# Transposing the last two blocks' normalised tiles: from TensorE to 32x32 squares by DMA and VectorE, with three sums of w2's rows at other units

## The chip, the cores and the metric

The kernel runs on one core of a Trainium2 chip. Its time is the device time of one execution in microseconds (us). The time before is the median of three runs. A profile is one further execution, recorded instruction by instruction; it has a time of its own, and a span from its first to its last instruction.

## The reference, cut to what matters

One transformer block with modulation, on x of 2048 tokens by 512 channels, all in float32:

```
mod = silu(c) @ w_mod -> sa, ca, ga, sb, cb, gb          # six rows of 512
h = layernorm(x) * (1 + ca) + sa
x = x + ga * (linear_attention(h @ wqkv) @ wo)           # 32 heads of 16
h = layernorm(x) * (1 + cb) + sb
x = x + gb * (mish(h @ w1 + b1) @ w2)                    # 512 -> 1792 -> 512
```

The change is about the second layernorm's h, on its way into `h @ w1`, and about w2.

## The kernel before

**Blocks and passes.** The 2048 tokens are four blocks of 512, each of four tiles of 128 tokens by 512 channels. `b` names the block, `t` the tile of tokens, `j` a group of 128 channels, `f` one of the 14 groups of 128 hidden columns of w1 (`NF`), `g` a pair of these (7, `G`). All matrix products run on TensorE in pieces of float32r: each operand is split into a high half (ScalarE, L82) and a low half (VectorE, L88), and `mm3` (L72) makes three matmuls of a product. Several products use seven multiplications in place of eight; that is why sums and differences of operands are prepared (`rows` for w1, `columns` for the normalised activations, `w2_sums` for w2's rows).

**The MLP.** Blocks 0 and 1 go through `h @ w1` together, then blocks 2 and 3. `pair_unit` (L1146) does one pair `g` for two blocks at once: seven products of six matmuls, and two `between` units. For blocks 0 and 1 the pairs run in the loop at L1244. Beside them `trail(f)` (L1230) multiplies the finished hidden columns of block 0 with w2 (`d_unit`, L1067, twelve matmuls). After the loop come the trails of f = 11, 12, 13 (L1258), and then `second(1, prepare)` (L1261): fourteen units of twelve matmuls each for block 1, in the order `last_first` (f = 10 to 13, then 0 to 9). `prepare(f)` (L1201) is called at the start of each such unit. Then the last stage begins: `pair_begin` and `two_pairs` for blocks 2 and 3 (L1382), and the w2 products of these blocks.

**The normalised tiles of blocks 2 and 3.** `norm_tile(b, t)` (L918) normalises one tile of tokens in place and stores it to a DRAM tile `nd` (POOL's queue, L937), two tiles in each of the units g = 2 to 5. After the last pair of the loop, `load_back` (L939) loads the eight tiles again as `nb` (SP's queue). The product with w1 needs them with channels on partitions. `transpose_f` (L945) does that: four TensorE transposes of 128x128 into one PSUM bank, then one ScalarE activation that applies scale and shift and writes `hf`. `prepare` calls it twice in each of the units 1, 3, 5 and 7 of `second`. In units 4 and 8 it starts `columns`, which reads four `hf` each and makes the operands of the seven products.

**Sums of w2's rows.** `w2_sums(g)` (L695) loads two row groups of w2 from DRAM (`w2p`, L700) where `g` is below 5, makes four differences on VectorE (L710), splits them, and stores the halves to DRAM (`w2t`, L726, four stores on SP). `W2_AT` (L693) says in which unit of `second` which `g` is started. `load_wt` (L1348) reads `w2t` when the seventh pair of the last stage begins and later.

**Order.** The instructions of each engine run in the order in which this program issues them. Side work is written as generators: `spawn` adds one that advances at every `tick`, up to its next `yield`; `spawn_idle` adds one to a list of which only the first two (three in the last stage) advance. So `prep_a` (L1178), which splits the activations for `second`, puts its ScalarE half into one tick and its VectorE half into the next. SBUF tiles come from one pool of 101 buffers; a tile waits for the last use of the buffer that it is given.

Of the kernel before, what the change touches and what calls it, by code (L numbers as in the profile page):

```python
# [8 lines left out]
F32 = mybir.dt.float32  # L9
# [4 lines left out]
P = 128  # L14
# [11 lines left out]
def block_kernel(ctx: ExitStack, tc: tile.TileContext, x, wqkv, wo, w1, b1t, w2, c, wmodt, out):  # L26
# [11 lines left out]
    def sb(name, dt=F32, shape=(P, 512)):  # L38

        return big.tile(list(shape), dt, tag="T", name=name, bufs=SLOTS)  # L40
# [12 lines left out]
    def spawn_idle(gen):  # L53

        idle_work.append(gen)

    def tick():

        running.extend(fresh)
        fresh.clear()  # L60
        for g in list(running):
            if next(g, "end") == "end":
                running.remove(g)
        for g in idle_work[:width[0]]:
            if next(g, "end") == "end":
                idle_work.remove(g)
# [623 lines left out]
            pool.dma_start(w2f[g][:, n, :], t)  # L690

    w2t, w2k, wb = {}, {}, {}
    W2_AT = {0: 6, 1: 5, 2: 0, 3: 1, 6: 2}  # L693

    def w2_sums(g):  # L695

# [43 lines left out]
    def rows(g, wait):  # L740

        r = [sb(f"w1p_{g}_{i}", F32, (P, 4, P)) for i in range(2)]
        for i in range(2):
            f = 2 * g + i
            sp.dma_start(r[i], w1[:, P * f:P * (f + 1)].rearrange("(k p) f -> p k f", p=P))
        for _ in range(wait):
            yield
        a11, a12, a21, a22 = [r[i][:, 2 * k:2 * k + 2, :] for i in range(2) for k in range(2)]
        s12, s34 = [sb(f"s{n}_{g}", F32, (P, 4, P)) for n in (12, 34)]
        s1, s2, s3, s4 = s12[:, 0:2, :], s12[:, 2:4, :], s34[:, 0:2, :], s34[:, 2:4, :]  # L750
        dve.tensor_tensor(s1, a21, a22, op=ALU.add)
        dve.tensor_tensor(s2, s1, a11, op=ALU.subtract)
        dve.tensor_tensor(s3, a11, a21, op=ALU.subtract)
        dve.tensor_tensor(s4, a12, s2, op=ALU.subtract)
        yield
        keep, todo = {}, []
        op_rows[g] = keep
        for name, v, parts in (("a1", r[0], ("a11", "a12")), ("s12", s12, ("s1", "s2")), ("s34", s34, ("s3", "s4")),
                               ("a22", a22, ("a22",))):
            half = split(f"{name}_{g}", v, keep, name)  # L760
            next(half)
            todo.append((name, half, parts))
            if len(todo) == 2:
                yield
                for name, half, parts in todo:
                    run(half)
                    for i, part in enumerate(parts):
                        op_a[g, part] = [h[:, 2 * i:2 * i + 2, :] for h in keep[name]]
                todo = []
# [148 lines left out]
    def norm_tile(b, t):  # L918

        v = xt.pop(("r", b, t))  # L920
        if t % 2:
            ln_stats("n", b, t, v)
            ln_eps("n", b, t, t + 1)
            ln_rstd("n", b, t, t + 1)
            yield
            ln_apply("n", b, t, v, v, dve)
        else:
            sums = act_sums("n", b, t, v)
            yield
            sums_eps("n", b, t, sums)  # L930
            yield
            sums_shift("n", b, t, sums)
            yield
            ln_apply("n", b, t, v, v, act)
        yield
        d = nd[b, t] = drp.tile([P, D], F32, name=f"nd_{b}_{t}")
        pool.dma_start(d, v)  # L937

    def load_back(key, src, b, t):  # L939
        v = xt[key, b, t] = sb(f"{key}b_{b}_{t}")  # L940
        sp.dma_start(v, src.pop((b, t)))

    hf, op_b = {}, {}

    def transpose_f(b, j, ptag="tp"):  # L945
        p = ps(ptag, f"tp_n_{b}_{j}")
        for t in range(4):
            pe.transpose(p[:, P * t:P * (t + 1)], xt["n", b, t][:, P * j:P * (j + 1)], ident)  # L948
        hf[b, j] = sb(f"hf_n_{b}_{j}")
        act.activation(hf[b, j], p, AF.Identity, bias=mc[:, 12 + j:13 + j], scale=mc[:, 16 + j:17 + j])  # L950
# [4 lines left out]
    def columns(c0, c, done):  # L955

        b11, b12, b21, b22 = [hf.pop((b, c + h)) for h in (0, 2) for b in (c0, c0 + 1)]
        t = [sb(f"t_{c0}_{c}_{i}") for i in range(4)]
        for d, u, v in (t[0], b12, b11), (t[1], b22, t[0]), (t[2], b22, b12), (t[3], b21, t[1]):
            dve.tensor_tensor(d, u, v, op=ALU.subtract)  # L960
        yield
        names = [("b11", b11), ("b21", b21), ("t1", t[0]), ("t2", t[1]), ("t3", t[2]), ("t4", t[3]), ("b22", b22)]
        halves = [split(f"{name}_{c0}_{c}", v, op_b, (name, c)) for name, v in names if name not in done]
        for n in range(0, len(halves) + 2, 2):
            for h in halves[max(n - 2, 0):n] + halves[n:n + 2]:
                next(h, None)
            yield
# [132 lines left out]
    def pair_begin(c0, g, tags):  # L1100

        u1, pa = sb(f"u1_{g}"), product(g, "a11", "b11", tags[0])
        act.activation(u1, pa, AF.Copy)  # L1103
        c11, p = sb(f"c11_{g}"), product(g, "a12", "b21", tags[1])

        def result():
            add(c11, p, u1)
            yield
            yield from mish(c11, c0, 2 * g)

        spawn(result())
        return pa
# [33 lines left out]
    def pair_unit(c0, g, odd, between):  # L1146
        begun = pair_begin(c0, g, ("tp" if odd else "h", "h"))
        tick()
        state = pair_early(g, begun, "h")
        tick()  # L1150
        between[0]()
        pair_middle(g, *state)
        tick()
        between[1]()
        tick()
        pair_end(c0, g, *state)
# [39 lines left out]
            spawn(prep_a(b, last_first[u - NF + 3]))  # L1196

    G = NF // 2
    order = [(b, c + h) for c in range(2) for h in (0, 2) for b in (2, 3)]

    def prepare(f):  # L1201

        if f in (1, 3, 5, 7):
            for _ in range(2):
                transpose_f(*order.pop(0), "h")
        if f in (4, 8):
            spawn_idle(columns(2, f // 4 - 1, ()))
        if f in W2_AT:
            spawn(w2_sums(W2_AT[f]))
        if f == NF - 2:  # L1210
            load_rows(0)
            load_wb(5)
        if f == NF - 1:
            load_wb(6)
# [11 lines left out]
    def norm_next():  # L1226
        if tiles:
            spawn(tiles.pop(0))

    def trail(f, side=None, norm=True):  # L1230
        def unit():
            if side is not None:
                if norm:
                    norm_next()
                spawn(side)
            d_unit(0, f, f)
            ahead(1, f)
            if f > 5 and f % 2 == 0:
                for i in (4, 5):
                    if f + i < NF:  # L1240
                        load_w2(f + i)
        return unit

    for g in range(1, G):  # L1244
        for f in (2 * g, 2 * g + 1):
            spawn(w2_job(f))
        if g == 1:
            two_pairs(0, 0, 1, begun, (lambda: None, trail(0, rows(3, 2), False)))
            store_rows(0)
        else:  # L1250
            norm_next()
            pair_unit(0, g, g % 2, (trail(2 * g - 3), trail(2 * g - 2, rows(g + 2, 2) if g + 2 < G else ())))
        if g < KEPT:
            store_rows(g)
        if g == G - 1:
            for n in range(8):
                load_back("n", nd, 2 + n // 4, n % 4)
    for f in (NF - 3, NF - 2, NF - 1):  # L1258
        trail(f)()
        tick()  # L1260
    second(1, prepare)  # L1261


# [98 lines left out]
    for n, g in enumerate(pairs):  # L1362
        if n < 5:
            if n:
                load_rows(n)
            if n:
                load_wb(pairs[n + 1])
        if n == 5:
            load_wb(pairs[6])
            load_r(0, 0)  # L1370
        if n == 6:
            for m in pairs[:5]:
                load_wt("m4", m)
        def gap(c, m):
            def unit():
                e_unit(c, m)
            return unit

        if n in (3, 5):
            spawn_idle(w2_sums(SUMS_KEPT[n // 2 - 1]))  # L1380
        if n == 0:
            begun = [pair_begin(L, pairs[i], ("tp" if i else "h", "acc")) for i in range(2)]  # L1382
            tick()
        elif n == 1:
            two_pairs(L, pairs[0], g, begun, (gap(0, 0), gap(0, 1)))
            for i in range(2):
                spawn_idle(left_trail(pairs[i]))
        else:
            pair_unit(L, g, n % 2, (gap(1, 0), gap(1, 1)) if n == 2 else (gap(0, n - 1), gap(1, n - 1)))
            if n < EARLY:  # L1390
                spawn_idle(left_trail(g))
# [70 lines left out]
```

## Time and profile before

| what | value |
|---|---|
| median of 3 runs | 493.3 us (493.01 to 493.44) |
| the profiled execution, its own time | 493.66 us |
| its span | 492.0 us |
| granted TensorE clock | 1.00 |
| busy: POOL / ScalarE / VectorE / TensorE | 146.1 / 296.4 / 370.8 / 487.3 us |
| moved by DMA | 98.58 MB in 66785 packets |
| unit g = 6 of the first pass | from about 286.3 to 301.3 us |
| trails of f = 11, 12, 13 | to 309.3 us |
| `second(1, prepare)` | 309.3 to 351.0 us |

In the profile, PE is TensorE, PEld its weight loads, DVE VectorE, ACT ScalarE, POOL GpSimd, SP SyncE; L948 is line 948. q0 is the DMA queue of POOL, q1 that of SP. A row of a timeline gives start, duration, engine, line, operation, output and input, and in brackets how long the engine was idle before and what ended that. A row of the windows gives for a stretch of time its length, then the busy time of PE, PEld, DVE, ACT and POOL with the number of instructions, the granted clock, the mean busy share of the 16 DMA engines (records overlap, so it can exceed 1), and GB/s; where it is asked for one engine, only that engine's. A row of waits gives who waited for whom, the total, the number of times and the longest.

### The profile page before, as it was taken

The numbers are of one execution on the slowest core, as the hardware profiler recorded it, in microseconds if no ns is written. First come the engines' busy times: TensorE is split into PE (matmuls) and PEld (weight loads), VectorE is DVE, ScalarE is ACT, GpSimd is POOL, SyncE is SP. The second block draws the span as 40 slices with busy tenths as digits, with TensorE's granted clock in tenths as the row PEclk, the third lists the DMA queues.
The fourth block names the chain that finished last, engine by engine and source line by source line (L and its number), as shares of the span: only waits on it lengthen the run. The fifth ranks groups of instructions, "written<-read, shape, count | busy, mean of one in ns | idle before, by whom it ended". The sixth has DMA issues, their size and how long they took to land.

```text
span 492.0 us, 7721 instructions
## 1 busy us (share of the span) xinstructions
PE 487.3 (99%) x2642; PEld 411.7 (84%) x2642; DVE 370.8 (75%) x717; ACT 296.4 (60%) x530; POOL 146.1 (30%) x244
## 2 busy tenths in 40 slices
PE   8999999999999999999999999999999999999997
PEld 7788888878878888888888888888888888899997
DVE  7988888999799698976877653789732666769872
ACT  6768587866546879738767655288045555668100
POOL 4583120000022123103432336114744410545200
PEclk9999999999999999999999999999999999999999
DMA  8815554244864417488899879999997803688512
GB/s 306 294 43 119 138 128 86 56 148 145 290 168 108 128 45 244 130 282 294 279 328 360 295 233 284 297 293 368 385 300 193 228 24 114 176 212 244 120 44 87
DMA packets 66785, 98.58 MB, mean 200 GB/s; under 512 B 7057, under 2 KB 31641, under 8 KB 66746
## 3 DMA queue, kind: packets, MB, share of 16 engines
q0 software_dynamic: 28704, 44.19, 32.8%
q1 hardware_dynamic: 37896, 53.63, 32.5%
q8 instruction: 21, 0.34, 0.3%
q10 hardware_dynamic: 146, 0.26, 0.2%
q14 instruction: 18, 0.15, 0.1%
HBM read 62.92 MB, written 33.03 MB: 195 GB/s over the span
## 4 chain that ended last, share of the span: by engine, by line
PE 96%; DVE 2%; ACT 1%; POOL 0%; ACTq 0%; issue 0%
PE p_a L1093 19%; PE p_s L1093 8%; PE oacc L75 5%; PE oacc L76 5%; PE oacc L74 5%; PE m L76 5%; PE m L75 5%; PE m L74 5%; PE o L74 3%; PE o L76 3%; PE o L75 3%; PE pq_a L371 3%; PE gacc L74 2%; PE gacc L76 2%; PE pk L76 2%; PE gacc L75 2%
## 5 line engine op out<-in xcount | busy, mean ns | idle before, releaser
L205 POOL TENSOR_TENSOR rs_n<-rs_n,half 128x1 f32<-128x1 f32 x16 | 11.4, 712 | 61.5 <-DVE rs_n L200 35.5
L1098 DVE TENSOR_TENSOR cb<-p_s,u 128x512 f32<-128x512 f32 x28 | 19.2, 687 | 13.2 <-ACT u L1134 13.2
L1128 ACT ACTIVATE u<-p_a 128x512 f32<-128x512 f32 x12 | 7.2, 599 | 28.8 <-PE p_a L1093 28.8
L1103 ACT ACTIVATE u<-p_a 128x512 f32<-128x512 f32 x14 | 8.4, 598 | 25.8 <-PE p_a L1093 25.8
L1085 ACT ACTIVATE ub<-cb,b1c 128x512 f32<-128x512 f32 x28 | 20.0, 717 | 4.9 <-DVE cb L1098 4.7
L1360 POOL DMA_DIRECT2D wt_m<-w2t x20 | 14.0, 704 | 26.8 <-DVE cb L1098 14.7
L950 ACT ACTIVATE hf_n<-tp_n,mc 128x512 f32<-128x512 f32 x16 | 11.7, 769 | 12.8 <-PE tp_n L948 12.8
L1134 ACT ACTIVATE u<-p_a 128x512 f32<-128x512 f32 x14 | 8.4, 598 | 17.0 <-PE p_a L1093 16.0
L738 POOL DMA_DIRECT2D w2b<-w2d x20 | 10.6, 540 | 23.9 <-DVE a_12l L88 5.0
L1098 DVE TENSOR_TENSOR c<-p_a,u 128x512 f32<-128x512 f32 x14 | 9.6, 689 | 8.6 <-PE p_a L1093 6.0
L850 POOL DMA_DIRECT2D rden_d<-rden x2 | 1.4, 720 | 45.7 <-DVE rden L848 45.7
L265 DVE SCALAR_TENSOR_TENSOR ku<-e_k,relu_k 128x512 f32<-128x512 f32 x15 | 10.7, 715 | 4.9 <-ACT relu_k L263 4.8
L732 POOL DMA_DIRECT2D wb<-w2d x14 | 9.9, 712 | 14.8 <-PE p_a L1093 12.4
L1062 ACT ACTIVATE u<-p_a,b1c 128x512 f32<-128x512 f32 x14 | 9.6, 687 | 6.9 <-PE p_a L1093 6.9
L262 ACT ACTIVATE e_k<-pk 128x512 f32<-128x512 f32 x15 | 8.9, 591 | 7.8 <-PE pk L76 7.8
L205 POOL TENSOR_TENSOR rs_x<-rs_x,half 128x1 f32<-128x1 f32 (+1 forms) x10 | 7.4, 746 | 19.6 <-DVE rs_x L200 18.4
L265 DVE SCALAR_TENSOR_TENSOR q<-e_q,relu_q 128x512 f32<-128x512 f32 x16 | 10.7, 684 | 3.1 <-ACT relu_q L263 3.1
L214 ACT ACTIVATE x<-x,nb_x,rs_x 128x512 f32<-128x512 f32 x13 | 10.0, 809 | 4.7 <-DVE nb_x L209 4.0
L274 POOL DMA_DIRECT2D ku<-ku x8 | 7.2, 901 | 17.6 <-DVE ku L265 17.6
L874 DVE TENSOR_TENSOR r<-o,r 128x512 f32<-128x512 f32 x16 | 10.8, 676 | 1.0 <-PE o L76 0.9
L862 DVE SCALAR_TENSOR_TENSOR q<-q,rd 128x512 f32<-128x512 f32 x16 | 10.4, 684 | 1.5 <-DMA rd<-rden_d 1.5
L785 POOL DMA_DIRECT2D a1b<-rd_a x10 | 5.4, 541 | 18.5 <-PE p_a L1093 8.1
(1620 smaller groups left out, 1972.3 us busy)
## 6 DMA issues: line engine op xcount, KB each, us to landing
wm<-in_wmodt_dram SPq DMA_DIRECT2D x24, 256.0 KB, 5.4
w2b<-w2d POOLq DMA_DIRECT2D x20, 256.0 KB, 5.4
wt_m<-w2t POOLq DMA_DIRECT2D x20, 256.0 KB, 3.9
r<-in_x_dram SPq DMA_DIRECT2D x16, 256.0 KB, 3.0
x<-in_x_dram SPq DMA_DIRECT2D x15, 256.0 KB, 4.8
w1p<-in_w_dram SPq DMA_DIRECT2D x14, 256.0 KB, 4.0
w2r<-in_w_dram SPq DMA_DIRECT2D x14, 256.0 KB, 5.9
wb<-w2d POOLq DMA_DIRECT2D x14, 256.0 KB, 5.4
```

The costliest lines, as they stand in the source:

```text
L74: pe.matmul(o, st[0], mv[0], start=start, stop=False)
L75: pe.matmul(o, st[0], mv[1], start=False, stop=False)
L76: pe.matmul(o, st[1], mv[0], start=False, stop=stop)
L205: pool.tensor_tensor(y, y, half[:, lo:hi], op=ALU.pow)
L265: dve.scalar_tensor_tensor(dst, e, 1.0, r, op0=ALU.min, op1=ALU.add)
L371: pe.matmul(p, l, r, start=onto is None and c == 0 and i == 0, stop=c == 1 and i == 2, skip_group_check=onto is not None)
L874: dve.tensor_tensor(r, p, r, op=ALU.add)
L950: act.activation(hf[b, j], p, AF.Identity, bias=mc[:, 12 + j:13 + j], scale=mc[:, 16 + j:17 + j])
L1085: act.activation(u, p, AF.Mish, bias=b1c[:, f:f + 1])
L1093: pe.matmul(p, st, mv, start=onto is None and c == 0 and i == 0, stop=c == 1 and i == 2, skip_group_check=onto is not None)
L1098: dve.tensor_tensor(out, p, u, op=ALU.add)
L1360: pool.dma_start(v, w2t[g][:, :, SUM[name], :])
```

## The change

The tiles of one block go to one DRAM tile of 512 tokens. `load_squares(b)` reads them again in 16 DMAs for each block: a DMA fills 32 partitions of a tile `y` with 16 squares of 32x32, so that one VectorE transpose, which turns every 32x32 square in its place, gives the tile with channels on partitions (`turn`). ScalarE applies scale and shift in place. Block 2 is read before the last pair of the first pass, block 3 after it. The eight `turn`s start two in each of the trails of f = 11, 12 and 13, and one in each of the units 0 and 1 of `second`. `columns` starts in units 2 and 6. Sums 0 and 1 of w2's rows move from units 2 and 3 to 9 and 11 of `second`; sum 2 moves from unit 6 to the beginning of the last stage.

```diff
-    W2_AT = {0: 6, 1: 5, 2: 0, 3: 1, 6: 2}
+    W2_AT = {0: 6, 1: 5, 9: 0, 11: 1}
...
-        d = nd[b, t] = drp.tile([P, D], F32, name=f"nd_{b}_{t}")
-        pool.dma_start(d, v)
-
-    def load_back(key, src, b, t):
-        v = xt[key, b, t] = sb(f"{key}b_{b}_{t}")
-        sp.dma_start(v, src.pop((b, t)))
-
-    hf, op_b = {}, {}
+        if t == 0:
+            nd[b] = drp.tile([512, D], F32, name=f"nd_{b}")
+        pool.dma_start(nd[b][P * t:P * (t + 1), :], v)
+
+    hf, op_b, yd = {}, {}, {}
+
+    def load_squares(b):
+        for j in (0, 2, 1, 3):
+            y = yd[b, j] = sb(f"y_{b}_{j}")
+            for c in range(4):
+                lo = P * j + 32 * c
+                sp.dma_start(y[32 * c:32 * (c + 1), :].rearrange("q (m r) -> q m r", r=32),
+                             nd[b][:, lo:lo + 32].rearrange("(m q) r -> q m r", q=32))
+
+    def turn(b, j):
+        v = hf[b, j] = sb(f"hf_n_{b}_{j}")
+        dve.transpose(v, yd.pop((b, j)))
+        yield
+        act.activation(v, v, AF.Identity, bias=mc[:, 12 + j:13 + j], scale=mc[:, 16 + j:17 + j])
...
-    order = [(b, c + h) for c in range(2) for h in (0, 2) for b in (2, 3)]
+    order = [(b, j) for b in (2, 3) for j in (0, 2, 1, 3)]
+
+    def turn_next():
+        if order:
+            spawn(turn(*order.pop(0)))
 
     def prepare(f):
 
-        if f in (1, 3, 5, 7):
-            for _ in range(2):
-                transpose_f(*order.pop(0), "h")
-        if f in (4, 8):
-            spawn_idle(columns(2, f // 4 - 1, ()))
+        turn_next()
+        if f in (2, 6):
+            spawn_idle(columns(2, f // 4, ()))
...
             norm_next()
+            if g == G - 1:
+                load_squares(2)
             pair_unit(0, g, g % 2, (trail(2 * g - 3), trail(2 * g - 2, rows(g + 2, 2) if g + 2 < G else ())))
         if g < KEPT:
             store_rows(g)
-        if g == G - 1:
-            for n in range(8):
-                load_back("n", nd, 2 + n // 4, n % 4)
+    load_squares(3)
     for f in (NF - 3, NF - 2, NF - 1):
         trail(f)()
+        turn_next()
+        turn_next()
         tick()
     second(1, prepare)
...
         if n == 0:
+            spawn_idle(w2_sums(2))
             begun = [pair_begin(L, pairs[i], ("tp" if i else "h", "acc")) for i in range(2)]
```

## The prediction

> **What bounds the kernel now.** I read the page first (busy shares, then the chain that ended last), then TensorE's own waits, then the stage that the diff touches, cut into units.
>
> ```profile
> span 492.0 us, 7721 instructions
> ...
> PE 487.3 (99%) x2642; PEld 411.7 (84%) x2642; DVE 370.8 (75%) x717; ACT 296.4 (60%) x530; POOL 146.1 (30%) x244
> ...
> PE 96%; DVE 2%; ACT 1%; POOL 0%; ACTq 0%; issue 0%
> ```
>
> ```profile
> PE warm L139 <- POOL ones L131: 1.1, 1, 1.1
> PE gacc L308 <- POOL pk_2h L84: 0.2, 1, 0.2
> ```
>
> TensorE is busy 99% of the span, the chain runs 96% through it, and in the whole run it waits twice, 1.3 us together, both long before the stage in question. So an instruction that leaves TensorE gives back its issue time, and a delay elsewhere costs something only once TensorE starts to wait for it. The change must be judged by both: what TensorE is spared, and whether the new route is in time.
>
> What the transposes cost is not their listed duration, since matmuls overlap. The windows of `second(1, prepare)`, one per unit of twelve matmuls, show it; four of the eight also hold eight transposes.
>
> ```profile
> 312.02:315.64 3.62, 3.62 (x21) 1.00 1.00 293
> 315.64:318.37 2.73, 2.73 (x14) 1.00 0.81 278
> 318.37:322.00 3.63, 3.63 (x21) 1.00 0.56 161
> 322.00:324.73 2.73, 2.73 (x14) 1.00 1.01 374
> 324.73:328.33 3.60, 3.60 (x21) 1.00 0.91 225
> 328.33:331.06 2.73, 2.73 (x14) 1.00 0.99 317
> 331.06:334.68 3.62, 3.62 (x21) 1.00 0.99 369
> 334.68:337.40 2.72, 2.72 (x13) 1.00 1.09 371
> ```
>
> ```profile
> L948 PE MATMUL tp_n<-ident,nb x32: 270/272/276, 312.0 to 331.8; 128*128 128x128 f32 x32
> ...
> L950 ACT ACTIVATE hf_n<-tp_n,mc x16: 759/768/783, 182.5 to 332.6; 128x512 f32<-128x512 f32 x16
> ```
>
> With transposes: 3.62 + 3.63 + 3.60 + 3.62 = 14.47 us. Without: 2.73 + 2.73 + 2.73 + 2.72 = 10.91 us. The difference, 3.56 us for 32 transposes (0.11 us each), is all that the change can give, at a granted clock of 1.00 in all eight windows.
>
> **The change part by part.** *Removed from TensorE:* the 32 transposes, 3.56 us, all on the path.
>
> *ScalarE:* the same eight scalings, now from SBUF. The row gives 0.77 us from PSUM; I take the same. They run earlier, in the trailing units 11 to 13 and units 0 to 2 of `second`, where the stage table below shows ScalarE with time to spare (2.84 of 8.20 us busy).
>
> *VectorE:* eight 32x32 transposes of 128x512, an operation that this trace doesn't have. Bounds: the 128x256 addition below (0.42 us) and ScalarE's 0.77 us; I take the 128x512 subtraction, 0.69 us, so 5.5 us in all. Six are queued during units 11 to 13, two in units 0 and 1.
>
> ```profile
> 286.30:301.30 15.00, 15.00 (x68) 12.43 (x67) 5.77 (x9) 6.66 (x12) 5.96 (x12) 1.00 0.96 309
> 301.30:309.50 8.20, 8.20 (x37) 6.78 (x37) 4.03 (x7) 2.84 (x6) 3.81 (x8) 1.00 1.07 307
> 309.50:320.40 10.90, 10.90 (x57) 9.17 (x56) 6.64 (x15) 3.88 (x7) 2.12 (x4) 1.00 0.85 275
> 320.40:331.30 10.90, 10.90 (x55) 9.09 (x54) 10.12 (x20) 9.11 (x18) 2.12 (x4) 1.00 0.95 293
> 331.30:342.20 10.90, 10.90 (x54) 9.12 (x53) 10.77 (x21) 9.71 (x18) 4.54 (x9) 1.00 1.03 361
> 342.20:351.20 9.00, 9.00 (x41) 7.47 (x40) 9.00 (x16) 1.16 (x3) 5.91 (x11) 1.00 1.27 382
> 351.20:363.40 12.20, 12.20 (x55) 10.10 (x54) 4.08 (x7) 4.77 (x8) 7.80 (x15) 1.00 1.27 385
> ```
>
> The columns are PE, PEld, DVE, ACT, POOL, clock, DMA share, GB/s. VectorE has 4.2 us free in 301.30 to 309.50 and 4.3 us in the next row, so the transposes themselves fit. Between 320 and 351 it is nearly full (29.9 of 30.8 us); there the moves of `w2_sums` take work away, so what is hidden now stays hidden.
>
> *The moves:* sums 0 and 1 go from units 2 and 3 to 9 and 11, sum 2 from unit 6 to the beginning of the last pair's stage. One sum is four additions of 0.42 us and four subtractions of 0.69 us on VectorE, 4.4 us end to end. The cover of sum 2 is 351.20 to 363.40, where VectorE works 4.08 of 12.20 us. Its results (`w2t`) are read by `load_wt` only when that stage's seventh pair begins. Each sum brings six DMAs of 256 KB on SP, two loads and four stores: sums 0 and 1 move behind the stores of sums 6 and 5, sum 2 behind the last four stores of `out`; nothing on SP waits for them in turn. They are 1.5 MB each, 3.9 us at the 385 GB/s of the last row, where the DMA share is 1.27, so POOL's loads there get later. The nearest of these is `wb`:
>
> ```profile
> 345.23 2.11 POOL L732 DMA_DIRECT2D wb<-w2d  x3 [0.17 <-DVE a_8l L88]
> ```
>
> TensorE first reads it at 365.98 (row below), 18 us after the last issue, so even two sums ahead of it are covered. I cost the moves at nothing; without their covers they would cost 4.4 us of VectorE each. `columns` starts two units earlier, also at nothing.
>
> *The squares:* eight loads of 256 KB become 32 of 64 KB, each of 512 pieces of 128 bytes. This is the disputed cost. The old loads and their waits on SP:
>
> ```profile
> 277.93 0.33 SPq L669 DMA_DIRECT2D w2r<-in_w_dram  x1
> 287.73 7.12 SPq L941 DMA_DIRECT2D nb<-nd  x8
> ```
>
> ```profile
> SPq L941 <- PE p_a L1093: 10.9, 4, 9.4
> ...
> SPq L941 <- DMA nd<-r: 2.1, 1, 2.1
> ```
>
> SP is free from 278.3 and then sits 9.4 us for a buffer that a product of unit 6 frees at 287.7. The new `load_squares(2)` stands one unit (15.0 us, the first row of the stage table) earlier in the program, so the buffer it gets was freed about a unit earlier, and it should start near 278.3. `load_squares(3)` needs all of block 3, which landed at about 294.5 (the last of the eight loads, issued then, followed the wait of 2.1 us).
>
> No 128-byte load is in this trace. The nearest by number of pieces is `w1p`: 512 pieces of 512 bytes per DMA. Its own rows, and a window in which it runs alone; then the two queues:
>
> ```profile
> L745 SPq DMA_DIRECT2D w1p<-in_w_dram x14: 378/384/1375, 96.5 to 264.5; - x14
> ...
> DMA to landing us min/median/max: 3.4/4.0/6.3
> ```
>
> ```profile
> q1 hardware_dynamic: 639, 0.32, 57.9%
> ```
>
> ```profile
> q1 hardware_dynamic: 37896, 53.63, 32.5%
> ```
>
> ```profile
> q0 software_dynamic: 2016, 3.67, 71.9%
> ```
>
> In 97.0 to 98.9 us a 512-byte piece took 0.579 x 16 x 1.9 / 639 = 27.5 ns of an engine. A square has 32 pieces per engine, so one square takes d = 0.88 us at that price. The lower bound is SP's issue time, 0.38 us; the upper is the mean piece of SP's queue over the whole run, 0.325 x 16 x 492.0 / 37896 = 67.5 ns, d = 2.16 us. I take 0.88, the nearest row, as a ceiling for the likely case, since a shorter piece should not take longer.
>
> When must they be there? VectorE takes its instructions in order, and behind the transposes are the splits that TensorE needs:
>
> ```profile
> 303.97 0.69 DVE L88 TENSOR_TENSOR a_10l<-ub,a_10h 128x512 fp32r<-128x512 f32 x1 [1.31 <-ACT a_10h L82]
> 307.46 2.73 DVE L1077 TENSOR_TENSOR r<-oacc,r 128x512 f32<-128x512 f32 x4 [2.79 <-PE oacc L76]
> 310.10 0.68 DVE L88 TENSOR_TENSOR a_11l<-ub,a_11h 128x512 fp32r<-128x512 f32 x1
> ...
> 361.27 0.69 DVE L88 TENSOR_TENSOR a_10l<-u,a_10h 128x512 fp32r<-128x512 f32 x1 [3.88 <-ACT a_10h L82]
> ```
>
> ```profile
> 309.30 0.39 PE L74 MATMUL oacc<-w_10h,a_10h 128*128 128x512 f32 x1
> ...
> 322.00 0.39 PE L74 MATMUL oacc<-w2b,a_0h 128*128 128x512 f32 x1
> ...
> 365.98 0.28 PE L74 MATMUL m<-wb,a_10h 128*128 128x256 f32 x1
> ```
>
> Block 2's four transposes stand ahead of `r<-oacc` (307.46), `a_10l` and `a_11l`; block 3's ahead of `a_12l`, `a_13l` and `a_0l`. Without transposes on TensorE, unit 4 of `second`, which reads `a_0l`, starts at 309.30 + 4 x 2.73 = 320.2 instead of 322.0. The last square's transpose and `a_0l` take 1.4 us, so the last square must land by about 318.5. Issued back to back it lands at 278.3 + 31d + 4.0, or, if block 3's landing sets the start, 294.5 + 15d + 4.0. At d = 0.88: 309.6 or 311.7, 7 us to spare. It fails from d = 1.17 on.
>
> A second claim on the same engines: the last fence of the four is POOL's queue in 294.5 to 312.0 us, 0.719 x 17.5 = 12.6 us per engine. If all of it went ahead of block 3's squares (14.1 us at d = 0.88), the last would land near 321, some 3 us late; at d = 0.42 it would be near 314, in time.
>
> The Trainium skill, "DMA: Bandwidth & Descriptors", section Specifications, says that transfers reach line rate from 512 bytes on and that below it a DMA engine reads, modifies and writes. No run here shows 128-byte pieces; if that doubled the 27.5 ns, d would be an estimated 1.76 us and the kernel slower, as in rival A.
>
> **Sum.** 493.66 us, the profiled execution (span 492.0 and 1.66 around it), less 3.56 gives 490.1. The median of the three runs shown, 493.3, lies 0.36 lower; from it the forecast is 489.7.
>
> **The rivals.**
>
> *A, the squares come late (slower).* Mechanism: small pieces hold SP's transfers up, VectorE stands in its queue at a transpose, the split behind it is late and TensorE waits at units 1 to 4. It decides from d = 1.17; the gain is used up at 1.17 + 3.56 / 31 = 1.28 us. At the upper bound, d = 2.16, the last square lands at 278.3 + 31 x 2.16 + 4.0 = 349.3, unit 4 starts at 350.7 instead of 320.2: 489.7 + 30.5 = 520. For it: nothing here measures 128-byte pieces. Against: 512-byte pieces took less time than the mean piece, so time falls with size. Another page of the Trainium skill, "VectorE: DVE Perf Modes", section The three transpose paths, warns that a plain DMA that transposes by strides is 19 times slower than the hardware's transpose where the innermost destination stride is large; these squares keep runs of 32 elements on both sides, so its condition isn't met.
>
> *B, contention eats part.* d near 0.88 and POOL's loads of `w2b` ahead: up to about 3 us late, 490.5 to 493.5.
>
> *C, sum 2 in the last stage.* If all its 4.4 us stood ahead of `a_10l` (done at 361.96, read at 365.98, 4.0 us to spare), TensorE would lose 0.4 us: about 490.1.
>
> *D, the change saves nothing.* This would need TensorE to wait elsewhere for what it is spared. The waits of 1.3 us speak against it: in the stage from 351.20, VectorE and ScalarE work 4.08 and 4.77 of 12.20 us. It would give 493.3.
>
> **How the numbers follow.** Forecast 0.57 (489.2 to 490.5); A 0.25; B 0.12; C 0.04; D 0.02. About 0.2% (1 us) is what a measurement of this kernel can tell from no change. Faster by more: 0.57 + 0.04 + half of B = 0.67. Within: the other half of B and D, 0.08. Slower: A, 0.25. The range runs from 489.0 (a little more saved than the windows show) to 499.0, which takes in B, C, D and the milder part of A (499 is d = 1.17 + 9.3 / 31 = 1.47); about 0.18 lies outside.
>
> **What would show it.** Right: no L948 instructions after 300 us, units of 2.73 us throughout `second`, TensorE's waits unchanged, eight VectorE transposes near 0.7 us, squares landing before 318. Wrong: a wait of TensorE for a VectorE split `a_10l` to `a_0l` with VectorE itself waiting for a DMA of `y` (A or B, by its length); or a wait at the first `m<-wb` products (C).

## The result and the profile after

| | before | after |
|---|---|---|
| median, us (6 runs each) | 493.33 (493.01 to 493.44) | 489.63 (489.3 to 490.06) |
| ratio to before, 95% interval | 1 | 0.9926 [0.9913, 0.9939] |
| the profiled execution, us | 493.66 | 489.74 |
| its span, us | 492.0 | 488.0 |

The change takes 3.7 us off, as forecast (489.7 against 489.63). The busy times of the page of after, the share of its chain, and below them all waits of TensorE:

```profile
span 488.0 us, 7703 instructions
...
PE 483.4 (99%) x2610; PEld 408.6 (84%) x2610; DVE 375.8 (77%) x725; ACT 296.8 (61%) x530; POOL 145.9 (30%) x244
...
PE 96%; DVE 2%; ACT 1%; POOL 0%; ACTq 0%; issue 0%
```

```profile
PE warm L139 <- POOL ones L131: 1.1, 1, 1.1
PE gacc L308 <- POOL pk_2h L84: 0.2, 1, 0.2
PE tp_late L502 <- ACT x L214: 0.2, 1, 0.2
```

TensorE has 32 instructions fewer and is as full as before; the one new wait, 0.2 us, is in the first ten microseconds of the span, far from the change. VectorE has eight instructions more and 5.0 us more work. The four units of `second` that held transposes, in the windows of after for TensorE, and the first matmuls of `second` and of the last stage in its timeline:

```profile
311.70:314.42 2.72, 2.72 (x13) 1.00 1.13 362
...
317.15:319.87 2.72, 2.72 (x14) 1.00 0.49 169
...
322.60:325.33 2.73, 2.73 (x14) 1.00 0.93 276
...
328.05:330.77 2.72, 2.72 (x14) 1.00 1.10 383
```

```profile
308.99 0.39 PE L74 MATMUL oacc<-w_10h,a_10h 128*128 128x512 f32 x1
...
347.06 0.39 PE L1107 MATMUL p_a<-b_0h,a_5h 128*128 128x512 f32 x1
```

Units 1, 3, 5 and 7 are now like the others. The stage takes 347.06 - 308.99 = 38.07 us instead of 351.00 - 309.30 = 41.70: 3.63 us, against 3.56 forecast. It starts 0.31 us earlier, and that is not the change's: 0.3 us are there in the two traces at 200 us already.

The new route, in after's groups of the turns (L955: count, nanoseconds, first and last start), in its timeline of SP, and in its DMA table from 280 to 290 us:

```profile
L955 DVE STREAM_TRANSPOSE hf_n<-y x8: 668/702/705, 302.3 to 313.8; 128x512 f32<-128x512 f32 x8
```

```profile
279.26 22.51 SPq L949 DMA_DIRECT2D y<-nd  x32
```

```profile
q1 hardware_dynamic: 7931, 0.99, 65.0%
```

A transpose on VectorE takes 0.70 us and never waits for its squares. The 32 transfers are issued from 279.26 to 301.8; in between, SP waits 4.3 us for the last store of block 3, so that block 3's begin at 292.5. A piece of 128 bytes takes 0.65 x 16 x 10 / 7931 = 13.1 ns of a DMA engine, half of the 27.5 ns that the prediction worked out for the 512-byte piece of `w1p`.

The stage table of after, with the columns and order of the prediction's:

```profile
301.00:309.00 8.00, 8.00 (x37) 6.60 (x37) 6.27 (x10) 5.13 (x9) 2.66 (x6) 1.00 1.39 309
309.00:319.90 10.90, 10.90 (x50) 9.03 (x49) 10.48 (x21) 7.22 (x12) 3.71 (x7) 1.00 0.92 288
319.90:330.80 10.90, 10.90 (x50) 9.03 (x49) 10.87 (x19) 8.54 (x16) 2.64 (x5) 1.00 0.96 284
330.80:341.70 10.90, 10.90 (x50) 9.03 (x49) 10.87 (x21) 4.12 (x8) 8.08 (x14) 1.00 1.12 339
341.70:347.10 5.40, 5.40 (x26) 4.46 (x25) 3.62 (x8) 0.00 (x0) 4.07 (x9) 1.00 1.14 313
```

The third busy figure is VectorE's: 10.48 + 10.87 + 10.87 + 3.62 = 35.84 of the 38.1 us of `second`. It is full for 33 us on end and has its longest pause near the end. The profile doesn't say whether that matters, since no one waits; the experiments do.

### The profile page after: what moved, and what is told of

Read it like the earlier page. It is cut to its first block, busy times and chain, and to the rows that moved or that the text cites. A ratio compares the mean times of both kernels' runs of the same rounds, so it can differ in the third digit from the quotient of the medians.

```text
span 488.0 us, 7703 instructions
## 1 busy us (share of the span) xinstructions
PE 483.4 (99%) x2610; PEld 408.6 (84%) x2610; DVE 375.8 (77%) x725; ACT 296.8 (61%) x530; POOL 145.9 (30%) x244
## 4 chain that ended last, share of the span: by engine, by line
PE 96%; DVE 2%; ACT 1%; POOL 0%; ACTq 0%; issue 0%
PE p_a L1107 20%; PE p_s L1107 8%; PE oacc L76 5%; PE oacc L75 5%; PE oacc L74 5%; PE m L76 5%; PE m L75 5%; PE m L74 5%; PE o L74 3%; PE o L76 3%; PE o L75 3%; PE pq_a L371 3%; PE gacc L74 2%; PE gacc L76 2%; PE pk L76 2%; PE gacc L75 2%
## 5 line engine op out<-in xcount | busy, mean ns | idle before, releaser
L265 DVE SCALAR_TENSOR_TENSOR ku<-e_k,relu_k 128x512 f32<-128x512 f32 x15 | 10.7, 715 | 4.9 <-ACT relu_k L263 4.7
L265 DVE SCALAR_TENSOR_TENSOR q<-e_q,relu_q 128x512 f32<-128x512 f32 x16 | 10.7, 685 | 3.1 <-ACT relu_q L263 3.1
L879 POOL DMA_DIRECT2D x1d<-r x8 | 4.4, 549 | 20.9 <-DVE r L874 20.9
```

What stands on the lines that cost most here:

```text
L265: dve.scalar_tensor_tensor(dst, e, 1.0, r, op0=ALU.min, op1=ALU.add)
```

## The experiments

The theory: the gain is the transposes' issue time on TensorE, and it is kept because the squares land in time. The rivals: something else moved (the sums, or VectorE's own load) makes or breaks it. All ratios are to the kernel before, run on the same chip.

**1. The squares alone, the moves alone.** The first kernel is after with the three sums left where they were:

```diff
-    W2_AT = {0: 6, 1: 5, 9: 0, 11: 1}
+    W2_AT = {0: 6, 1: 5, 2: 0, 3: 1, 6: 2}
...
-            spawn_idle(w2_sums(2))
```

> The changed kernel with the sums of w2's rows left where they were (sums 0, 1 and 2 in units 2, 3 and 6 of second). Theory A (the whole gain is TensorE's 3.56 us; the moves only keep VectorE's queue free): VectorE worked 35.8 of 38.1 us between 309.0 and 347.1 in the changed kernel; sum 2 brings 3.8 us back into that stretch, 39.6 of 38.1, so TensorE waits somewhere for a split, 0 to 2 us in all: 489.6 to 491.6, most likely 490.5. Rival B (the moves are not needed at all): 489.6, no wait of TensorE. Rival C (the moves carry the gain): near 493.3.

The second is before with these two edits the other way round: the sums are moved and nothing else.

> The kernel before with only the three sums of w2's rows moved. Theory A: TensorE does what it did and waited for nothing before, so no change: 493.3 within 0.3. Rival C (the moves carry part of the gain): below 492.5. Sum 2 in the last stage too dear: above 493.7, with a wait of TensorE at the first products of the last stage.

Measured: squares alone 495.05 us (493.33 to 495.92), ratio 1.0027 [1.0017, 1.0038]; moves alone 493.41, ratio 1.0002 [0.9993, 1.001]. The moves give nothing by themselves, and without them the whole gain is gone: 5.4 us lie between after and the squares alone, a loss that neither text expected (the highest forecast for the first kernel was near 493.3). The new waits of TensorE in the squares alone:

```profile
PE oacc L76 <- DVE a_5l L88: 2.5, 1, 2.5
...
PE oacc L76 <- DVE a_3l L88: 0.3, 1, 0.3
```

It waits for VectorE, and VectorE there for nothing. Two stretches of VectorE's timeline show what it does, first in the squares alone, then in after; both run from the split of a_1 to that of a_5:

```profile
320.62 0.69 DVE L88 TENSOR_TENSOR a_1l<-ub,a_1h 128x512 fp32r<-128x512 f32 x1
...
322.42 0.42 DVE L710 TENSOR_TENSOR t<-w2p 128x256 f32<-128x256 f32 x1
...
328.97 2.49 DVE L88 TENSOR_TENSOR t_0l<-t,t_0h 128x512 fp32r<-128x512 f32 x4
...
336.92 0.68 DVE L88 TENSOR_TENSOR a_5l<-ub,a_5h 128x512 fp32r<-128x512 f32 x1
```

```profile
320.48 0.69 DVE L88 TENSOR_TENSOR a_1l<-ub,a_1h 128x512 fp32r<-128x512 f32 x1
...
331.44 0.68 DVE L88 TENSOR_TENSOR a_5l<-ub,a_5h 128x512 fp32r<-128x512 f32 x1
```

16.30 us against 10.96. Between the two splits stand, in the squares alone, eight additions (L710) and four splits of sums 0 and 1 more; at the distances of their starts that is 2 x 1.47 + 4 x 0.60 = 5.3 us, the whole difference. `a_5l` is then 2.5 us late. That these 5.3 us are nearly the 5.4 of the medians is chance: in the profile `second` lasts 41.84 us (309.12 to 350.96), 3.8 more than in after, and the rest of the 5.4 is the subject of experiment 5.

**2. What the transposes cost.** Before, with the transposes on TensorE left out: ScalarE scales the tiles untransposed, so the transposition of blocks 2 and 3 is missing from the computation.

```diff
+    def scale_f(b, j):
+        hf[b, j] = sb(f"hf_n_{b}_{j}")
+        act.activation(hf[b, j], xt["n", b, j], AF.Identity, bias=mc[:, 12 + j:13 + j], scale=mc[:, 16 + j:17 + j])
...
-                transpose_f(*order.pop(0), "h")
+                scale_f(*order.pop(0))
```

> The kernel before, loads and sums as they were, with the 32 transposes of blocks 2 and 3 left out: ScalarE scales the untransposed tiles. This leaves out the transposition, and prices it alone. Theory A: 493.3 - 3.56 = 489.7, the same as the changed kernel within 0.4. Rival D (part of the changed kernel's gain comes from elsewhere, a smoother VectorE or DMA): 490.3 or more.

Measured: 490.12 us, ratio 0.9932 [0.992, 0.9944], 0.68% or 3.4 us less than before. That is 0.5 us above the 489.63 of after, and the two intervals overlap. `second` lasts 38.55 us (309.46 to 348.01), 3.15 less than before and 0.5 more than in after; it has one listed wait, for `a_7l`, 0.2 us. So nearly the whole gain of the change is there when the tiles are loaded as before and nothing is turned: it is TensorE's issue time.

**3. Amount or order on VectorE.** Four kernels between the squares alone and after. With `columns` back in units 4 and 8 and the sums not moved (their two edits are those of the first diff of experiment 1):

```diff
-        if f in (2, 6):
-            spawn_idle(columns(2, f // 4, ()))
+        if f in (4, 8):
+            spawn_idle(columns(2, f // 4 - 1, ()))
```

> The changed kernel with all three sums left where they were (units 2, 3, 6) and columns started in units 4 and 8 as before, not in 2 and 6. In the run with the squares alone VectorE was busy without a gap from 307.3 to 347.5 us and the split a_5l came 2.5 us late, behind two sums and both columns. Theory G (the order of VectorE's queue decides, not its amount: what is read late stood ahead of what is read soon): with columns later, a_5l comes forward, TensorE waits less than 1 us, 489.7 to 491. Rival H (the amount decides: VectorE has more to do in this stretch than TensorE leaves time for): TensorE waits some 2 to 3 us, there or at the beginning of the last stage, 492.5 to 496.

Measured: 491.48 us (490.33 to 491.61), ratio 0.9955 [0.9943, 0.9967]. VectorE has the same work in the stage, 37.53 us in either kernel, but TensorE's wait there is now 0.7 us, and for another split:

```profile
PE oacc L76 <- DVE a_7l L88: 0.7, 1, 0.7
```

`second` lasts 39.10 us (309.82 to 348.92), 1.0 more than in after. It also begins 0.8 us later than in after; that is a wait for `qs_2l` at 151.7 us, far ahead of anything that this edit touches. Then, with the new `columns`, only sum 2 moved (the first diff against after) and only sums 0 and 1 moved (the second):

```diff
-    W2_AT = {0: 6, 1: 5, 9: 0, 11: 1}
+    W2_AT = {0: 6, 1: 5, 2: 0, 3: 1}
```

```diff
-    W2_AT = {0: 6, 1: 5, 9: 0, 11: 1}
+    W2_AT = {0: 6, 1: 5, 6: 2, 9: 0, 11: 1}
...
-            spawn_idle(w2_sums(2))
```

> The changed kernel with sums 0 and 1 left in units 2 and 3 and only sum 2 moved to the last stage. With the squares alone, sum 2's additions stood behind a_5l. Theory G: moving sum 2 doesn't help, the wait for a_5l stays at 2.5 us: 493 to 495.5. Rival H: it takes 3.8 us of VectorE work out of the stretch, more than the wait: 489.6 to 490.5.

Measured: 494.94 us (493.44 to 495.46), ratio 1.0028 [1.0018, 1.0039]. TensorE's waits and the end of `second` in the windows:

```profile
PE oacc L76 <- DVE a_5l L88: 2.5, 1, 2.5
...
PE oacc L76 <- DVE a_3l L88: 0.3, 1, 0.3
```

```profile
341.70:347.10 5.40, 5.40 (x25) 4.49 (x24) 2.90 (x5) 0.00 (x0) 3.47 (x7) 1.00 1.41 357
```

VectorE now has 2.5 of 5.4 us free at the end, and the wait for `a_5l` is the same 2.5 us. So for this wait it is not the amount of work in the stage that decides, but what stands in front of `a_5l`.

> The changed kernel with sums 0 and 1 moved to units 9 and 11 and sum 2 left in unit 6. Theory G: what stood ahead of a_5l is gone, no wait there; VectorE ends the stretch with a backlog that is read late: 489.6 to 490.6. Rival H: the amount in units 4 to 13 is higher than in the changed kernel by 3.8 us, and TensorE waits late in second or at the first sums of the last stage: 491.5 or more.

Measured: 496.46 us (494.12 to 498.13), ratio 1.0062 [1.004, 1.0083]; expected was the gain or nearly all of it. The wait for `a_5l` is gone. A short one (0.4 us, for `a_6l`) and a long one are there instead: TensorE's long wait, VectorE's, and SP's timeline, of this kernel:

```profile
PE p_a L1107 <- DVE r L1091: 4.2, 1, 4.2
```

```profile
350.28 0.43 DVE L710 TENSOR_TENSOR t<-w2p 128x256 f32<-128x256 f32 x1 [3.28 <-DMA w2p<-w2f]
```

```profile
336.60 0.32 SPq L726 DMA_DIRECT2D w2t<-t_2h  x1
...
342.18 1.36 SPq L700 DMA_DIRECT2D w2p<-w2f  x2
```

SP issues sum 1's loads at 342.18, behind the four stores of sum 2; in after all four loads of sums 0 and 1 go out from 326.92 to 330.3. VectorE stands at sum 1's additions until the loads have landed (the first addition is at 350.28, the second waits to 351.72), and `r<-oacc`, for which the last stage's second product waits, is queued behind them; its first product runs at 347.77. So in this trace sum 2 has to leave `second` too for SP's queue rather than for VectorE's time. Sum 1's loads ahead of those stores were not tried. Last, all sums moved as in after, with the old `columns`:

> The changed kernel, but columns starts in units 4 and 8 of second as before; the three sums stay moved. If the moves of the sums alone make the room on VectorE and the columns' place matters only beside sums that were not moved: no wait for a_3l, a_5l or a_7l of more than 0.3 us, 489.3 to 490.3. Rival (later columns push work in front of the last r and the last stage's splits, which already end with 1.7 us to spare): a wait at the first products of the last stage or for a_7l, 0.5 to 3 us: 490.3 to 493.

Measured: 489.88 us (489.43 to 490.42), ratio 0.9929 [0.9914, 0.9944], with no new wait in the stage. The four kernels together, with the new route in all of them:

| | `columns` in units 4 and 8 | in units 2 and 6 |
|---|---|---|
| sums not moved | 491.48 | 495.05 |
| sums moved | 489.88 | 489.63 |

The medians give the moves of the sums 1.6 us with the old `columns` and 5.4 us with the new. In the profiles, where what lies ahead of the stage can be left out, the moves shorten `second` by 1.0 us (39.10 to 38.08) and by 3.8 us (41.84 to 38.07). The place of `columns` is worth nothing once the sums are out of the way.

**4. When the squares are too late.** Four kernels put the squares off. Each square loaded three times (the last time into `y`), each one twice, each read in two halves of 64-byte pieces, and the squares of block 2 issued after the last pair of the first pass instead of before it:

```diff
+            spare = [sb(f"spare{i}_{b}_{j}") for i in range(2)]
...
-                sp.dma_start(y[32 * c:32 * (c + 1), :].rearrange("q (m r) -> q m r", r=32),
-                             nd[b][:, lo:lo + 32].rearrange("(m q) r -> q m r", q=32))
+                for i in range(3):
+                    z = y if i == 2 else spare[i]
+                    sp.dma_start(z[32 * c:32 * (c + 1), :].rearrange("q (m r) -> q m r", r=32),
+                                 nd[b][:, lo:lo + 32].rearrange("(m q) r -> q m r", q=32))
```

```diff
+                for h in (0, 16):
+                    sp.dma_start(y[32 * c:32 * (c + 1), :].rearrange("q (m r) -> q m r", r=32)[:, :, h:h + 16],
+                                 nd[b][:, lo + h:lo + h + 16].rearrange("(m q) r -> q m r", q=32))
```

```diff
-            if g == G - 1:
-                load_squares(2)
...
+    load_squares(2)
     load_squares(3)
```

The first diff is that of three times (twice has one `spare`, `range(2)` and `i == 1`), the second that of the halves, the third that of the later squares.

> The changed kernel with every square loaded three times, the third time into the tile that is used. 96 transfers on SP at 0.55 to 0.58 us each instead of 32. Theory A with the deadline rule (the last square must land some 1.7 us before unit 4 of second starts at 319.9): block 2's issued from 279.3 to 305.7, block 3's to 333.5, landed at 335.7, unit 4 late by 335.7 + 1.4 - 319.9 = 17 us: 506 to 508. Rival E (late squares are mostly absorbed, since VectorE has other work and TensorE's queue is deep): under 495. Rival F (the pieces crowd POOL's loads out as well): over 512.

> The changed kernel with every square loaded twice, the second time into the tile that is used. With three loads the 96 transfers took 65 us on SP, 0.68 each (0.53 where no other queue moved anything, about 2 beside POOL's loads of w2b). At 0.68 the 64 end at 322.8 and land near 325; unit 4 of second should start at 319.9 and can then start at 326.5: 6.6 us late, 496 if TensorE's clock holds, up to 500 if the wait costs clock as it did with three loads. If the rule of the deadline is wrong (late squares are absorbed): 489.6 to 491. In time if the pace is 0.57: 489.6.

> The changed kernel with each square read in two halves: 64 transfers of 32 KB, each of 512 pieces of 64 bytes; as many pieces and transfers as with every square loaded twice, but half of those bytes. If the number of transfers and pieces sets SP's pace: about the time of squares loaded twice (504.8), with the last issue near 328 and waits of TensorE of about 10 us; 502 to 506. If the bytes set it: the pace of the changed kernel's squares for the same bytes, 32 x 0.55 us of SP, and no new wait: 489.3 to 491.

> The changed kernel, but block 2's squares are issued after the last pair of the first pass, in front of block 3's. Margin theory (a square only has to land before VectorE's queue lets a_0l slip past about 318 us, and alone a transfer takes 0.55 us of SP): they start at about 288 instead of 279.3, all 32 are issued by 306 to 309, the last lands before 315, TensorE waits for nothing new: 489.3 to 490.3. Rival (the pace beside POOL's loads of w2b, some 2 us for each transfer between 299 and 311, holds for all that is left by then): block 3's sixteen run until about 320 or later, VectorE waits for y, and TensorE waits 1 to 6 us for a_12l or a_0l: 491 to 497.

| | transfers, first to last issue | VectorE waits for squares | new waits of TensorE | median, us | ratio |
|---|---|---|---|---|---|
| after | 32, 279.3 to 301.1 | 0 | 0 | 489.63 | 0.9926 |
| later | 32, 287.5 to 315.6 | 7.0 | 2.6 | 497.7 (495.13 to 499.02) | 1.0081 [1.0049, 1.0112] |
| halves | 64, 279.6 to 324.5 | 12.7 | 6.6 | 501.99 | 1.0169 [1.0152, 1.0186] |
| twice | 64, 279.7 to 328.2 | 18.0 | 10.7 | 504.81 | 1.0229 [1.0216, 1.0242] |
| three times | 96, 279.3 to 344.6 | 37.3 | 25.3 | 524.11 | 1.062 [1.0606, 1.0634] |

The waits are those of the profiled executions. That of the later squares took 495.13 us, the other three 497.3 to 499.0; what makes these longer is open. In the squares loaded three times the profile puts 23.2 of VectorE's 37.3 us down to the extra transfers into `spare`.

In all of them the chain is the one that the prediction called rival A: VectorE stands at a transpose, what is queued behind it is late, TensorE waits. What is late is a split; in the squares loaded three times it is first `r<-oacc`, for 13.1 us. That kernel came out in the range of rival F of its expectation (over 512), but not by F's mechanism: POOL waits there 12.3 us for the transfers into `spare` before a load of `w2b`, yet TensorE waits for VectorE alone. VectorE's wait in the later squares, and TensorE's two in the squares loaded twice:

```profile
DVE hf_n L955 <- DMA y<-nd: 7.0, 3, 2.6
```

```profile
PE oacc L76 <- DVE a_12l L88: 8.1, 1, 8.1
PE oacc L76 <- DVE a_0l L88: 2.6, 1, 2.6
```

How late a square may be can be read from the later squares, in VectorE's timeline from the last transpose on, and in TensorE's:

```profile
320.80 0.71 DVE L955 STREAM_TRANSPOSE hf_n<-y 128x512 f32<-128x512 f32 x1 [2.64 <-DMA y<-nd]
...
322.53 0.42 DVE L710 TENSOR_TENSOR t<-t,w2r 128x256 f32<-128x256 f32 x1
322.86 0.68 DVE L88 TENSOR_TENSOR a_0l<-ub,a_0h 128x512 fp32r<-128x512 f32 x1
```

```profile
323.60 0.50 PE L76 MATMUL oacc<-w2b,a_0l 128*128 128x512 f32 x1 [2.33 <-DVE a_0l L88]
```

From the landing of the last square to the end of `a_0l` it is 2.7 us, since four additions (L710, sum 6) stand between the two. `second` begins at 309.10 in this kernel, so four undisturbed units of 2.73 us and two matmuls of 0.23 later this matmul would start at about 320.5: it is 3.1 us late, and the last square had to be there by about 317.7.

Twice and three times came out 5 to 18 us above what was expected of them, the later squares above the larger of their two forecasts. The halves come out near the squares loaded twice, which move twice the bytes in as many transfers: the number of transfers and pieces sets the pace, and the bytes do little (45 us for 64 transfers against 49). Besides the four additions two reasons for the excess can be read. The first is the pace, in SP's timeline of the later squares:

```profile
287.54 10.61 SPq L949 DMA_DIRECT2D y<-nd  x16
...
306.67 9.37 SPq L949 DMA_DIRECT2D y<-nd  x8
```

Sixteen transfers take 0.66 us each; from 306.67 on, beside POOL's loads of `w2b`, each takes 1.17. POOL's queue has 38.4% of the DMA engines' time in the first stretch (287.5 to 298) and 92.2% in the second (306.6 to 316). The expectations reckoned with the pace of the free queue (0.55) or counted too little of the slow stretch. After escapes the slowest stretch since its last square is issued at 301.1. The second reason is the clock.

**5. The wait's price.** Several kernels above are slower than their waits explain, and the times of some lie in two groups: six of the seven with only sum 2 moved from 494.78 to 495.46, and the profiled one at 493.44. A second execution of that kernel was profiled.

> The kernel with only sum 2 moved once more, for one further profiled execution. Its first profile took 493.44 us with a granted clock of 1.00 throughout, while six of its seven times lie from 494.78 to 495.46. Theory: the wait of 2.5 us for a_5l is in every execution, and in most of them a window of about 3.5 us follows at half the granted clock, which costs another 1.6 us; then an execution of 494.8 to 495.4 us has such a window within 4 us behind the wait, and the same wait of 2.5 us. Rival: the wait itself differs from execution to execution (about 4 us in a slow one), with the clock at 1.00. An execution of 493.4 us tells nothing.

This execution took 495.28 us, 1.84 more. First its wait and its windows for TensorE, then the same windows of the first profile:

```profile
PE oacc L76 <- DVE a_5l L88: 2.5, 1, 2.5
```

```profile
334.00:338.00 4.00, 1.47 (x7) 1.00 1.12 374
338.00:342.00 4.00, 4.00 (x12) 0.57 1.12 366
342.00:346.00 4.00, 4.00 (x20) 1.00 1.35 381
```

```profile
334.00:338.00 4.00, 1.47 (x6) 1.00 1.13 387
338.00:342.00 4.00, 4.00 (x19) 1.00 1.17 384
342.00:346.00 4.00, 4.00 (x20) 1.00 1.37 353
```

The wait is the same to the tenth. In the slower execution the clock then falls to half: 12 matmuls in four microseconds instead of 19, one every 0.43 us instead of every 0.23. A mean of 0.57 over 4 us is (1 - 0.57) x 2 x 4.0 = 3.4 us at half. `second` lasts 41.87 us in the first profile (308.88 to 350.75) and 43.46 in the second (309.10 to 352.56), against 38.07 in after. So the two listed waits, 2.8 us together, cost 3.8: a matmul is listed with 0.39 us although the next one normally begins 0.23 after it, and a wait is listed only from the end of these 0.39; behind the wait of 2.5 us the next matmul begins 0.34 later instead of 0.23. The half clock costs another 1.6. With both it is 5.4 us, the distance of the medians in experiment 1.

The half clock does not always last 3.4 us: in the halves, around a wait of 2.8 us, the granted clock is 0.50 from 329.0 to 335.5. The later squares have it behind a wait of 2.3 us, here in the windows of TensorE, and the squares loaded three times have it in several stretches, one of them here in a window of all engines:

```profile
323.60:328.20 4.60, 4.59 (x12) 0.63 0.36 115
```

```profile
324.00:328.00 4.00, 4.00 (x11) 3.03 (x11) 1.22 (x2) 0.81 (x1) 0.00 (x0) 0.50 0.78 123
```


## Why the prediction was right

- **The sum.** One term, TensorE's issue time of 32 transposes: 3.56 us forecast from the units with and without them, 3.63 measured in the stage, 3.4 on the whole time by leaving the transposes out. To read it from the windows and not from the listed 270 ns a transpose (8.6 us in all) was the step on which the number rests.
- **The transposes on VectorE.** 0.69 taken, 0.70 measured.
- **The squares.** SP was forecast to be free at 278.3; they start at 279.3. The taken ceiling of 27.5 ns a piece was twice the 13.1 measured, so the last square was in sooner than forecast. The price of 0.88 us a transfer was on the safe side of the 0.55 to 0.66 seen on the free queue, but not of the 1.17 beside POOL's loads, which is the very value from which the prediction said that it fails: the term had no price for a shared engine, only the later rival B. That it didn't matter here is due to the place of `load_squares(2)`. With the squares begun 8.3 us later the last of them was issued 14.5 us later and TensorE waited.
- **The deadline.** The prediction had only the transpose and the split between the last landing and `a_0l`, 1.4 us; the four additions of sum 6, which stand there too, make it 2.7 (experiment 4). So the last square had to land by about 317.7 and not by 318.5. In after it was issued at 301.1, and the slowest transfer took 5.5 us to land: it was there by 306.6, with some 11 us to spare where 7 were forecast. The missing term did no harm because the margin was wide, not because it was reckoned with.
- **Rival A** named the mechanism that the four late kernels show, and its rule for the delay (the last square's landing sets unit 4) holds in its order; its price left out sum 6's additions and the half clock behind a long wait.
- **The moves** were costed at nothing and are worth nothing alone. The sentence that with the moves "what is hidden now stays hidden" was the right one, but I had not worked out what would happen without them: 5.4 us, more than the whole gain. That the forecast did not need this number is luck: the change already held the moves. One sum was also put too high, at 4.4 us: it has two subtractions of 128x512 and not four, so it takes 1.47 + 2 x 0.60 = 2.7 us of VectorE. What it costs depends on the split that stands behind it in the queue. That the start of `columns` can be put at nothing held only because the sums moved.
- **Rival C** fell: TensorE has no wait in the last stage. **Rival D** fell with the units of 2.72 us.

The rule of the Trainium skill that the prediction weighed against the squares ("DMA: Bandwidth & Descriptors", section Specifications: below 512 bytes an engine reads, modifies and writes) doesn't show in these traces as a longer time for a piece; per byte the small pieces do cost more, 13.1 ns for 128 bytes against 27.5 for 512.

The Trainium skill, "TensorE: Matmul & The Clock Gate", section Part 1: The HAM clock gate, says that the clock falls to half after at least one idle window of about 3.4 us, and that the window runs freely. The half (a matmul every 0.43 us instead of 0.23) agrees with the traces, and the slow stretch lasted 3.4 us here. The length of the pause does not agree: 2.5 us was enough in one execution and not in the other, which is shorter than that sentence says. That the phase of the free window decides between the two would fit, but was not tried.

What stays open: the times of the squares alone also lie in two groups (three from 493.33 to 493.61, nine from 494.65 to 495.92). Their mean granted clocks fit the same half clock: 1.000 in the three, 0.996 or 0.997 in the nine, and 0.997 in the execution of 495.28 us whose slow window is shown above. None of the nine left a trace, so this is argued from the sister kernel. The 32 transposes of blocks 0 and 1 on TensorE (178.8 to 196.0 us) could perhaps be turned in the same way; VectorE is busy for 28.8 of the 30 us from 170 to 200 in after, and it wasn't tried.

## What to carry to other kernels

When TensorE never waits, work taken off it is worth its issue time, read from stretches with and without it, and the rest of the question is whether an in-order engine behind it has its operands in time. Look at what stands in that engine's queue in front of the next operand, not at its share of busy time: the same three sums cost nothing or 5.4 us by their place. Issue many small transfers before the other queue is busy (0.55 us each here, against 1.17). Put a wait of TensorE like the 2.5 us one here at some 0.3 us more than its listed length and, in some executions, at 1.6 us on top.

## What the hardware showed beyond the forecast

- The 128-byte pieces took 13.1 ns of a DMA engine, half of the 27.5 ns of the 512-byte pieces, and not twice as much; 64 transfers of half the bytes ran from 279.6 to 324.5, 64 of the full from 279.7 to 328.2.
- The granted clock falls to half for about 3.4 us after some waits of TensorE of 2.3 to 2.5 us; in the kernel with both profiles this adds 1.6 us to the stage, with the wait ahead of it the same to a tenth.
